# Token sums moved to VectorE, score blocks of 512 and 256 columns, and new numbers in a scheduling table, in a fused attention and two-layer feed-forward kernel

## The chip, the cores and the metric

The kernel runs on 1 core of one Trainium2 chip. The metric is the device time of one execution in microseconds (us). The time before is 764.21 us, the median of 3 runs (762.48 to 764.49). The profiler shows one execution on that core, engine by engine: TensorE (PE, and PEld for its weight loads), VectorE (DVE), ScalarE (ACT), GpSimd (POOL) and SyncE (SP, whose queue issues nearly all DMAs).

## The reference

Attention over 2 x 8 heads, 768 tokens, head size 64, where a query sees only keys of its own hash bucket (6 sign bits of a projection). Its output is 1536 tokens of 512 values, which pass through two feed-forward layers, each 512 to 2048 to 512. All in float32.

```python
mask = q_bucket[:, :, :, None] == k_bucket[:, :, None, :]
scores = np.where(mask, scale * q @ k.T, -1e9)
attn = np.exp(scores - max) / (sum + 1e-9)
x = (attn @ v)                       # as (1536, 512)
h = x @ w_in1;  x = (h * np.tanh(softplus(h))) @ w_out1
h = x @ w_in2;  out = (h - np.tanh(h)) @ w_out2
```

The weights w_in and w_out arrive as float64 (512 KB for each 128 x 512 tile) and are turned into float32 in the kernel.

## The kernel before

**Numbers in two parts.** A matrix product keeps float32 accuracy by splitting each operand into a rounded part and a remainder (names ending in h and l) and adding three products (L969 to L971, L1033, L1034, L1046), or two where one operand is exact.

**Attention.** Eight pairs of heads, one after the other. A pair's q, k and v are loaded, split (L404 to L424), and stacked by SP DMAs into operands a, b, c, d, in which the bucket's bits ride along. For each of 96 blocks of 128 queries TensorE makes 768 scores in four matmuls (L551, L552) into a PSUM tile `s` of two banks, with 384 columns in each bank. There is one such tile (`ps_s`, one buffer); three early blocks use two ordinary banks in its place (`SPLIT_S`). VectorE clamps the scores and takes their minimum (L555), ScalarE takes the exponential and the row sums (L577), TensorE transposes (L612), ScalarE rounds the result to `ph` (L628), VectorE makes the remainder `pl` (L631), and TensorE multiplies both with v (L590, L591). For some chunks GpSimd makes `ph` and `pl` (L355, L624). At the end of a half, 1/sum goes to DRAM and comes back spread over partitions (`inv`, `r`, L670, L674), and the result is scaled and split into `xh`, `xl` (L688 to L695).

**Feed-forward layers.** Each layer works on two halves of 768 tokens (one per batch entry), each in 8 units of 256 hidden columns. A unit's first product runs in seven block products in the manner of Strassen, from sums of weight blocks (`f`, L769) and sums of token blocks (t2, t3, t4, from the `tokens` function). In the first half of layer 1 it runs in eight plain products. The sums of tokens are 16 instructions per half (`whole` and `diff`, L855 and L858 in the source, recorded under the helper's line L769 as `t<-xh,xl` and `t<-t`), for three halves, all on GpSimd. Rounding a result is ACT work, its remainder (`gl`, `a`, `o`) VectorE work. The second product (L1033, L1034 in layer 1, L1046 in layer 2) sums over all units into six PSUM banks; its first two tiles are the two halves of the tile `s`. At the end `keep` writes xh and xl of layer 1, and `leave` copies each output tile out of PSUM (L1082) and sends it off.

**Weights.** `to_float` loads a float64 tile into a `raw` buffer (4 of them) and converts it: L792, L800 and L812 on VectorE, L808 on ScalarE. For the first two units of layer 1 the last step (L812) is GpSimd's; these eight tiles are converted during attention, one each 14 ticks of 1.13 us from tick 60 on (`CONV_A`, `CONV_S`). From the third unit on, the times follow the unit's own (`CONV1`), and all is VectorE's.

**What sets the order.** Every step is an `op` with an engine, a cost, a key (its due time) and a latency. `Plan.order` is a list scheduler: it plays the engines forward by these numbers, takes at each moment the op that can start first (lowest key among equals), and the instructions are then issued to each engine in that order. On the chip each engine runs its own list in order and waits at an instruction until its inputs and buffers are there. So a cost or latency in the table changes only the order. A DMA is an op of an engine "DMA" with cost max(0.55, bytes / 180e3 per us) and a latency of 2.1 us; on the chip that is the SP queue, which issues in order.

Of the kernel before, what the change touches and what calls it, by code (L numbers as in the profile page):

```python
# [30 lines left out]
U32 = mybir.dt.uint32  # L31
# [17 lines left out]
T_BUFS, P_BUFS, U_BUFS = 4, 6, 3  # L49
RAW_BUFS = 4  # L50

# [6 lines left out]
LATE = 0.22  # L58
# [20 lines left out]
RAW = 12.0  # L79
# [12 lines left out]
CONV2 = 6.0  # L92
N_PRE = 2
PLAIN = 8
TOK_A = 0.0
TOK_L = 75.0
TOK_S = 1.3
TOK_T = 3.0
CONV_A = 60
CONV_S = 14  # L100
CONV_R = 15.0
# [28 lines left out]
class Plan:  # L130


    LAT = {"PE": 0.2, "DMA": 2.1, "-": 0.0}

# [7 lines left out]
    def buf(self, pool, tag, shape, dtype=F32):  # L142
        return Buf(self, pool, tag, shape, dtype)

    def op(self, eng, cost, key, fn, reads=(), writes=(), after=(), release=0.0, lat=None):
        o = Op()
        o.lat = self.LAT.get(eng, LATE) if lat is None else lat
# [113 lines left out]
def tile_lsh_attention_moe(  # L261
# [96 lines left out]

    def dma(nbytes, key, out, in_, reads=(), writes=(), release=0.0, rate=180e3):

        op("DMA", max(0.55, nbytes / rate), key, lambda: nc.sync.dma_start(out=out(), in_=in_()), reads, writes, release=release)

# [173 lines left out]
    def scores(g, h, half, t, key):  # L536
# [4 lines left out]
        used = slice(0, NR + D) if g or h else slice(0, P)  # L541
        p, mn = buf("p", "p", [P, 2, HB]), buf("small", "mn", [P, 1])
        sm = sums[g, half]
        rows = (False, True) if g or h else (False, True, "bits")
        reads = [(x, y, half) for x in (a, c_) for y in rows]
        reads += [(x, y, i) for x in (b_, d_) for y in rows for i in range(2)]

        def products(outs):
            for kk, o in outs:
                kc = slice(kk * HB, (kk + 1) * HB)  # L550
                nc.tensor.matmul(o, a()[:, tok], b_()[:, kc], start=True, stop=False)  # L551
                nc.tensor.matmul(o, c_()[used, tok], d_()[used, kc], start=False, stop=True)  # L552
# [6 lines left out]
        if n in SPLIT_S:  # L559

            lows = []
            for kk in range(2):
                sc, low = buf("ps_t", "pt", [P, 512]), buf("small", "mn2", [P, 1])
                op("PE", 0.35, key, lambda sc=sc, kk=kk: products([(kk, sc()[:, :HB])]), reads, [sc])
                op("DVE", 0.47, key + 0.1, lambda sc=sc, kk=kk, low=low: clamp(p()[:, kk], sc()[:, :HB], low()), [sc], [(p, kk), low])
                lows.append(low)
            op(
                "DVE", 0.07, key + 0.15,
                lambda: nc.vector.tensor_tensor(out=mn(), in0=lows[0](), in1=lows[1](), op=ALU.min), lows, [mn],
            )  # L570
        else:
            sc = buf("ps_s", "s", [P, 2, 512])
            op("PE", 0.7, key, lambda: products([(kk, sc()[:, kk, 0:HB]) for kk in range(2)]), reads, [sc])
            op("DVE", 0.87, key + 0.1, lambda: clamp(p(), sc()[:, :, 0:HB], mn()), [sc], [(p, 0), (p, 1), mn])
        op(
# [23 lines left out]
    def chunk(g, h, half, c, ps, o, key, done):  # L599
# [9 lines left out]
        def transpose(ts):  # L609
            for t in ts:  # L610
                pc = ps[t]().rearrange("p a b -> p (a b)")
                nc.tensor.transpose(pt()[:, t * P:(t + 1) * P], pc[:, c * P:(c + 1) * P], ident)  # L612

        op("PE", 0.33, key, lambda: transpose(range(TB)), ps, [(pt, 0), (pt, 1)])
        if len(queue) >= PV_LAG:
# [34 lines left out]
    def inverse(g, half, key):  # L650
# [24 lines left out]

        op("DMA", 0.3, key + 0.3, store, [rt], [("inv", g, half)])
        op("DMA", 0.6, key + 0.4, spread, [("inv", g, half)], [r])

# [103 lines left out]
    def to_float(w, m, key, t, tok, lead=0.0, pooled=False):  # L782
# [3 lines left out]
        def word(i):  # L786
            return raw().bitcast(U32).rearrange("p (n t) -> p n t", t=2)[:, :, i]

        dma(P * DM * 8, key - RAW, raw, lambda: w[m], [], [raw], release=key - RAW - 4.0 - lead, rate=FAST)
        op(  # L790
            "DVE", 0.4, key,
            lambda: nc.vector.tensor_scalar(  # L792
# [41 lines left out]
    def tokens(layer, sb, keys, slack):  # L834
# [5 lines left out]
        for name in ("t2", "t3", "t4"):  # L840
            hl = [buf(f"t{sb + 1}", f"{name}{x}", [P, 2, HB], F32R) for x in "hl"]
            ops[name] = (lambda n, k, hl=hl: hl[n]()[:, k]), [(b, k) for b in hl for k in range(2)]
            more.append(hl)
        gate = [] if sb == 0 else ["wd"]
        for k in range(2):
            x = [buf("t", "t", [P, XB], F32) for i in range(4)]
# [6 lines left out]
            def whole(name, i, key, k=k, x=x, tmp=tmp):  # L853
                at_ = ops[name][0]
                op("POOL", 1.0, key, lambda: add(nc.gpsimd, tmp(i), at_(0, k), at_(1, k)), [*x_of(name), *gate], [x[i]], release=key - slack)  # L855

            def diff(i, a, b, key, x=x, tmp=tmp):
                op("POOL", 1.0, key, lambda: add(nc.gpsimd, tmp(i), tmp(a), tmp(b), True), [x[a], x[b]], [x[i]])  # L858

# [30 lines left out]
    def unit_weights(layer, sb, u, plain):  # L890
# [5 lines left out]
        for part in range(2):  # L896
# [3 lines left out]
            if (layer, sb) == (1, 0):  # L900
                for side in range(2):
# [3 lines left out]
                        weights[1][part], 2 * u + side, when,  # L905
                        lambda part=part, side=side: w32[part]()[:, side].bitcast(U32), (w32[part], side), lead=CONV_R if n < N_PRE else 0.0, pooled=n < N_PRE,
                    )
# [45 lines left out]
    def unit(layer, sb, u, ops):  # L953
# [7 lines left out]
        def product(a, b, bank, start, k):  # L961
# [10 lines left out]

            op("PE", 1.06, k, emit, [(tl, 0), (tl, 1), *toks], [bank])

# [3 lines left out]
        def act(src, m, i, k):  # L978
# [44 lines left out]
    def outer1(m, g, w, acc, key, d):  # L1023
# [26 lines left out]
    def keep(sb, acc, key):  # L1050

        for d in range(KD):
            for (a, n), cols, t0, nt in (
# [17 lines left out]
    def leave(sb, acc, key):  # L1071
        for t, (a, n_) in enumerate(acc):
# [120 lines left out]
```

## Time and profile before

| | before |
|---|---|
| median of 3 runs | 764.21 us |
| the profiled execution, its time | 763.45 us |
| its span, first to last instruction | 761.7 us |
| granted TensorE clock, mean | 0.997 |
| busy: PE, DVE, ACT, POOL | 743.0, 616.6, 513.9, 240.0 us |
| DMA moved | 111.09 MB |

The profiled execution took 763.45 us, 1.75 us more than its span; these lie around the first and last instruction. It is 0.76 us under the median of the three runs. Attention fills the span up to about 250 us (its last products stand beside the first unit of layer 1), layer 1 reaches to about 510 us and layer 2 to the end. A busy time is an average: where an engine is waited for is read from the idle time that stands in brackets behind a row of the timeline, and from the table of waits.

### The profile page before, as it was taken

The numbers are of one execution on the slowest core, as the hardware profiler recorded it, in microseconds if no ns is written. First come the engines' busy times: TensorE is split into PE (matmuls) and PEld (weight loads), VectorE is DVE, ScalarE is ACT, GpSimd is POOL, SyncE is SP. The second block draws the span as 40 slices with busy tenths as digits, with TensorE's granted clock in tenths as the row PEclk, the third lists the DMA queues.
The fourth block names the chain that finished last, engine by engine and source line by source line (L and its number), as shares of the span: only waits on it lengthen the run. The fifth ranks groups of instructions, "written<-read, shape, count | busy, mean of one in ns | idle before, by whom it ended". The sixth has DMA issues, their size and how long they took to land.

```text
span 761.7 us, 12370 instructions
## 1 busy us (share of the span) xinstructions
PE 743.0 (98%) x4189; PEld 678.2 (89%) x4189; DVE 616.6 (81%) x1220; ACT 513.9 (67%) x1076; POOL 240.0 (32%) x258
## 2 busy tenths in 40 slices
PE   7999999999997999999999999999999999999997
PEld 5898989999986999999999999998998898888986
DVE  6899999999999787877699999889987567665542
ACT  6999899999986765455575766666656455554541
POOL 5687697887745003700002231002530000000000
PEclk9999999999999999999999999999999999999999
DMA  6586686785452377525646555664312114120002
GB/s 175 146 209 173 160 207 195 199 203 152 108 168 95 115 252 231 190 107 191 217 162 210 190 191 211 223 205 138 111 56 83 56 56 167 64 75 28 28 0 83
DMA packets 40172, 111.09 MB, mean 146 GB/s; under 512 B 6310, under 2 KB 9254, under 8 KB 40108
## 3 DMA queue, kind: packets, MB, share of 16 engines
q1 hardware_dynamic: 39532, 109.67, 47.8%
q8 instruction: 33, 0.54, 0.3%
q10 hardware_dynamic: 576, 0.62, 0.2%
q14 instruction: 31, 0.25, 0.1%
HBM read 71.40 MB, written 19.97 MB: 120 GB/s over the span
## 4 chain that ended last, share of the span: by engine, by line
PE 85%; DVE 7%; DMA 3%; ACT 2%; issue 2%; POOL 0%; SPq 0%; ACTq 0%; POOLq 0%; DVEq 0%
PE pt L1046 11%; PE pt L969 10%; PE pt L971 10%; PE pt L970 10%; PE pt L612 7%; PE pt L1034 6%; PE s L1033 6%; PE pt L1033 5%; PE s L1046 5%; PE s L551 4%; PE s L552 3%; PE pt L590 3%; PE pt L591 3%; DVE p L555 2%; DVE pl L631 1%
## 5 line engine op out<-in xcount | busy, mean ns | idle before, releaser
L769 POOL TENSOR_TENSOR t<-xh,xl 128x384 f32<-128x384 f32 x24 | 42.5, 1774 | 254.0 <-DVE o L769 77.3
L969 PE MATMUL pt<-xh,a 128*128 128x384 f32 x320 | 108.2, 338 | 1.1 <-ACT pl L983 0.5
L971 PE MATMUL pt<-xh,a 128*128 128x384 f32 x320 | 107.9, 337 | 0.0
L970 PE MATMUL pt<-xl,a 128*128 128x384 f32 x320 | 107.8, 337 | 0.0
L577 ACT ACTIVATE p<-p,mn 128x768 f32<-128x768 f32 x96 | 90.5, 943 | 5.7 <-DVE p L555 3.9
L555 DVE TENSOR_SCALAR_CACHE_REDUCE p<-s 128x768 f32<-128x768 f32 x93 | 88.2, 949 | 7.0 <-PE s L552 6.1
L612 PE MATMUL pt<-cst,p 128*128 128x128 f32 x576 | 88.5, 273 | 3.4 <-ACT p L577 1.9
L612 PEld LDWEIGHTS pt<-cst,p 128*128 128x128 f32 x576 | 71.5, 140 | 11.7 <-ACT p L577 3.8
L631 DVE TENSOR_TENSOR pl<-pt,ph 128x384 fp32r<-128x384 f32 x148 | 78.0, 545 | 4.6 <-ACT ph L628 3.4
L769 DVE TENSOR_TENSOR gl<-pl,gh 128x384 fp32r<-128x384 f32 x128 | 73.5, 580 | 9.6 <-ACT gh L988 9.2
L1046 PE MATMUL pt<-o,gh 128*128 128x512 f32 x256 | 79.6, 392 | 0.0
L628 ACT CAST ph<-pt 128x384 fp32r<-128x384 f32 x148 | 67.8, 480 | 14.8 <-PE pt L612 6.9
L590 PE MATMUL pt<-ph,vt 128*128 128x384 f32 x192 | 72.0, 375 | 1.6 <-DVE pl L631 1.4
L551 PE MATMUL s<-b,a 128*128 128x384 f32 x186 | 68.7, 369 | 3.2 <-DVE p L555 3.0
L1034 PE MATMUL pt<-gh,o 128*128 128x256 f32 x256 | 71.7, 280 | 0.0
L988 ACT CAST gh<-pl 128x384 fp32r<-128x384 f32 x128 | 64.8, 512 | 7.4 <-DVE pl L769 6.7
L591 PE MATMUL pt<-pl,vt 128*128 128x384 f32 x192 | 65.3, 340 | 2.2 <-DVE pl L631 2.1
L969 PEld LDWEIGHTS pt<-xh,a 128*128 128x128 f32 x320 | 60.3, 189 | 6.6 <-DVE pl L769 0.9
L552 PE MATMUL s<-d,c 77*128 77x384 f32 (+1 forms) x186 | 63.2, 340 | 0.0
L970 PEld LDWEIGHTS pt<-xl,a 128*128 128x128 f32 x320 | 60.5, 189 | 1.8
L971 PEld LDWEIGHTS pt<-xh,a 128*128 128x128 f32 x320 | 60.5, 189 | 0.0
L769 DVE TENSOR_TENSOR pl<-pt,f 128x384 f32<-128x384 f32 x32 | 17.8, 556 | 46.8 <-ACT f L986 46.7
(154 smaller groups left out, 1960.4 us busy)
## 6 DMA issues: line engine op xcount, KB each, us to landing
w<-w SPq DMA_DIRECT2D x64, 512.0 KB
raw<-in_moe_w_in_dram SPq DMA_DIRECT2D x32, 512.0 KB
raw<-in_moe_w_out_dram SPq DMA_DIRECT2D x32, 512.0 KB
w<-t SPq DMA_DIRECT2D x32, 256.0 KB
b<-kh SPq DMA_DIRECT2D x30, 192.0 KB
v<-in_v_dram SPq DMA_DIRECT2D x8, 384.0 KB
r<-inv SPq DMA_DIRECT2D x32, 96.0 KB
a<-qh SPq DMA_DIRECT2D x15, 192.0 KB
```

Source lines behind the costliest of these rows:

```text
L551: nc.tensor.matmul(o, a()[:, tok], b_()[:, kc], start=True, stop=False)
L555: nc.vector.tensor_scalar(out=out, in0=in_, scalar1=MASKED, scalar2=None, op0=ALU.min, op1=ALU.min, accum_out=low)
L577: lambda: nc.scalar.activation(out=p(), in_=p(), func=AF.Exp, bias=mn(), scale=-1.0, accum_out=sm()[:, h, t:t + 1],),
L590: nc.tensor.matmul(o()[:, :HB], vt()[:, c, :], ph()[:, :HB], start=(c == 0), stop=False)
L591: nc.tensor.matmul(o()[:, :HB], vt()[:, c, :], pl()[:, :HB], start=False, stop=(c == NT - 1))
L612: nc.tensor.transpose(pt()[:, t * P:(t + 1) * P], pc[:, c * P:(c + 1) * P], ident)
L769: eng.tensor_tensor(out=out, in0=in0, in1=in1, op=ALU.subtract if sub else ALU.add)
L969: nc.tensor.matmul(o, tl()[:, 0, c], at_(0, kk), start=start and kk == 0, stop=False, skip_group_check=not start)
L970: nc.tensor.matmul(o, tl()[:, 0, c], at_(1, kk), start=False, stop=False, skip_group_check=not start)
L971: nc.tensor.matmul(o, tl()[:, 1, c], at_(0, kk), start=False, stop=kk == 1, skip_group_check=not start)
L1034: nc.tensor.matmul(r()[:, 0, rest], w()[:, y, c], flat[x][:, SEG:], start=st and d % 2 == 0, stop=sp, skip_group_check=True)
L1046: nc.tensor.matmul(o, x()[:, i, c], w()[:, y], start=m == 0 and k == 0, stop=m == KF - 1 and k == 2)
```

## The change

All sums of tokens are made on VectorE. A block's 768 scores are made as 512 and 256 columns, so that they lie without a gap in the two banks; the three early blocks that use ordinary banks are divided in the same way. In the last unit of a half the accumulators are finished in the order 0, 2, 1, 3, 4, 5, and copied out in that order. There are 5 `raw` buffers. The eight tiles converted during attention are due from tick 10 on, one each 22 ticks. In the table, DMA latency is 3.0 (a raw load's 4.0), the rate 250e3 bytes per us, and the four stores and two loads of `inv` count 1.3 and 1.2 for 0.3 and 0.6; a few costs of other ops change by some hundredths (such hunks are left out below).

```diff
-RAW_BUFS = 4
+RAW_BUFS = 5
+RAW_LAT = 4.0
+RATE, ISSUE = 250e3, 0.55
+C_STORE, C_SPREAD = 1.3, 1.2
+LAT_DMA = 3.0
+TOKS = ("DVE", 0.47)
...
-CONV_A = 60
-CONV_S = 14
+CONV_A = 10
+CONV_S = 22
...
+        parts = (slice(0, XB), slice(XB, S))
+
         def products(outs):
-            for kk, o in outs:
-                kc = slice(kk * HB, (kk + 1) * HB)
+            for kc, o in outs:
                 nc.tensor.matmul(o, a()[:, tok], b_()[:, kc], start=True, stop=False)
                 nc.tensor.matmul(o, c_()[used, tok], d_()[used, kc], start=False, stop=True)
...
-            op("PE", 0.7, key, lambda: products([(kk, sc()[:, kk, 0:HB]) for kk in range(2)]), reads, [sc])
-            op("DVE", 0.87, key + 0.1, lambda: clamp(p(), sc()[:, :, 0:HB], mn()), [sc], [(p, 0), (p, 1), mn])
+            flat = lambda: sc().rearrange("p a b -> p (a b)")
+            op("PE", 0.69, key, lambda: products([(kc, flat()[:, kc]) for kc in parts]), reads, [sc])
+            op("DVE", 0.87, key + 0.1, lambda: clamp(p(), flat()[:, :S], mn()), [sc], [(p, 0), (p, 1), mn])
...
-        op("DMA", 0.3, key + 0.3, store, [rt], [("inv", g, half)])
-        op("DMA", 0.6, key + 0.4, spread, [("inv", g, half)], [r])
+        op("DMA", C_STORE, key + 0.3, store, [rt], [("inv", g, half)])
+        op("DMA", C_SPREAD, key + 0.4, spread, [("inv", g, half)], [r])
...
+    LAST = (0, 2, 1, 3, 4, 5)
...
+        et = nc.vector if TOKS[0] == "DVE" else nc.gpsimd
...
-                op("POOL", 1.0, key, lambda: add(nc.gpsimd, tmp(i), at_(0, k), at_(1, k)), [*x_of(name), *gate], [x[i]], release=key - slack)
+                op(*TOKS, key, lambda: add(et, tmp(i), at_(0, k), at_(1, k)), [*x_of(name), *gate], [x[i]], release=key - slack)
...
-                op("POOL", 1.0, key, lambda: add(nc.gpsimd, tmp(i), tmp(a), tmp(b), True), [x[a], x[b]], [x[i]])
+                op(*TOKS, key, lambda: add(et, tmp(i), tmp(a), tmp(b), True), [x[a], x[b]], [x[i]])
...
-            k = key + 1.38 * t
+            k = key + 1.38 * LAST[t]
...
-                    k = key + dt * (n_out * i + t if u < NU - 1 else 2 * t + i)
+                    k = key + dt * (n_out * i + t if u < NU - 1 else 2 * LAST[t] + i)
```

The order that comes out differs in many places. Three of them follow, each before and after.

GpSimd before, from its last work of attention on: `ph` and `pl` are the last chunk's, and behind them stand the first sums of tokens, with nothing in between.

```order
L355 TENSOR_SCALAR ph<-f 128x384
L624 TENSOR_TENSOR pl<-f,ph 128x384
L769 TENSOR_TENSOR t<-xh_131,xl_135 128x384 x2
L769 TENSOR_TENSOR t<-t 128x384
L769 TENSOR_TENSOR t<-xh_133,xl_137 128x384
L769 TENSOR_TENSOR t<-t 128x384 x2
```

VectorE after, in layer 1: a piece of its list with two of these sums (`t<-xh,xl` and `t<-t`), among conversions of weights (L800, L808, L820) and remainders (`gl`, `o`).

```order
L777 TENSOR_TENSOR gl<-pl,gh 128x384
L800 TENSOR_SCALAR w_4824<-raw 128x512
L777 TENSOR_TENSOR o_4820<-w_4509,o_4820 128x512
L808 SCALAR_TENSOR_TENSOR w_4824<-raw,w_4824 128x512
L800 TENSOR_SCALAR w_4843<-raw 128x512
L777 TENSOR_TENSOR t<-xh_133,xl_137 128x384
L808 SCALAR_TENSOR_TENSOR w_4843<-raw,w_4843 128x512
L777 TENSOR_TENSOR t<-t 128x384
L777 TENSOR_TENSOR gl<-pl,gh 128x384
```

The sums have left GpSimd's list, which now ends with the last chunk's `pl`; on VectorE they stand in layer 1, behind the end of attention.

SyncE's queue from its first DMA on, before: the first pair's k and v, the stacking of `b`, and the second pair's k.

```order
L361 DMA k<-in_k_dram 128x384 x2
L361 DMA v<-in_v_dram 128x768
L361 DMA b<-kh 64x768 x2
L361 DMA k<-in_k_dram 128x768
L361 DMA a<-qh 64x768
L361 DMA q<-in_q_dram 128x768
```

The same place after:

```order
L367 DMA k<-in_k_dram 128x384 x2
L367 DMA v<-in_v_dram 128x768
L367 DMA raw<-in_moe_w_in_dram 128x512
L367 DMA b<-kh 64x768 x2
L367 DMA k<-in_k_dram 128x768
L367 DMA a<-qh 64x768
```

A raw load of 512 KB now stands ahead of the first stack and of the second pair's k.

TensorE's last unit, before: its first accumulators, of which the first two are halves of the tile `s` (o_9190 and o_9235 are the two weight tiles of the unit).

```order
L1046 MATMUL s<-o_9235,gh 128x512 x2
L1046 MATMUL s<-o_9235,gl 128x512
L1046 MATMUL s<-o_9190,gh 128x512 x2
L1046 MATMUL s<-o_9190,gl 128x512
L1046 MATMUL s<-o_9235,gh 128x512 x2
L1046 MATMUL s<-o_9235,gl 128x512
L1046 MATMUL pt<-o_9190,gh 128x512 x2
L1046 MATMUL pt<-o_9190,gl 128x512
```

And after:

```order
L1055 MATMUL s<-o_9235,gh 128x512 x2
L1055 MATMUL s<-o_9235,gl 128x512
L1055 MATMUL pt<-o_9190,gh 128x512 x2
L1055 MATMUL pt<-o_9190,gl 128x512
L1055 MATMUL pt<-o_9235,gh 128x512 x2
L1055 MATMUL pt<-o_9235,gl 128x512
L1055 MATMUL s<-o_9190,gh 128x512 x2
L1055 MATMUL s<-o_9190,gl 128x512
```

Between the first half of `s` and its second half now stand the six matmuls of an accumulator in another bank.

## Rows read from the trace of the kernel before

**Rows 1.** The page, part 1: busy us (share of the span) x instructions.

```profile
PE 743.0 (98%) x4189; PEld 678.2 (89%) x4189; DVE 616.6 (81%) x1220; ACT 513.9 (67%) x1076; POOL 240.0 (32%) x258
```

**Rows 2.** Windows: stretch, its length, busy us (instructions) by engine; PEclk; DMA.

```profile
core 0: us, PE busy (x) PEld busy (x) DVE busy (x) ACT busy (x) POOL busy (x), PEclk, DMA share, GB/s
0.00:16.00 16.00, 11.91 (x48) 8.29 (x49) 10.42 (x26) 9.73 (x18) 7.33 (x17) 1.00 0.71 197
16.00:236.00 220.00, 215.61 (x1386) 198.37 (x1384) 206.77 (x458) 202.33 (x443) 160.58 (x193) 1.00 0.65 167
236.00:247.00 11.00, 6.88 (x43) 5.74 (x41) 10.82 (x17) 5.34 (x13) 10.60 (x10) 1.00 0.45 142
247.00:262.00 15.00, 13.90 (x69) 13.58 (x70) 11.16 (x21) 10.00 (x20) 0.78 (x1) 0.89 0.39 133
400.00:460.00 60.00, 60.00 (x348) 56.30 (x347) 56.93 (x94) 39.42 (x83) 19.17 (x16) 1.00 0.61 200
520.00:560.00 40.00, 39.54 (x196) 35.02 (x195) 39.29 (x67) 23.82 (x50) 18.33 (x14) 1.00 0.36 119
```

**Rows 3.** Waits of PE from 236 to 258: total us, times, longest.

```profile
PE pt L591 <- DVE pl L631: 2.1, 1, 2.1
PE pt L590 <- DVE pl L631: 1.4, 1, 1.4
PE pt L612 <- DVE pl L631: 1.3, 1, 1.3
```

**Rows 4.** Timeline of DVE, 238 to 247: start us, us, instruction.

```profile
238.27 1.38 DVE L800 SCALAR_TENSOR_TENSOR w<-raw,w 128x512 uint32<-128x512 uint32 x1
...
239.70 1.10 DVE L792 TENSOR_SCALAR w<-raw 128x512 uint32<-128x512 uint32 x1
...
241.66 1.51 DVE L812 CUSTOM_DVE_ANT_0 w<-raw,w 128x1024 uint16<-128x1024 uint16 x1
...
244.25 1.40 DVE L800 SCALAR_TENSOR_TENSOR w<-raw,w 128x512 uint32<-128x512 uint32 x1
245.57 1.34 DVE L688 TENSOR_TENSOR u<-u,r 128x384 f32<-128x384 f32 x1
```

**Rows 5.** Timeline of POOL, first and last token sums of that stretch.

```profile
237.83 2.68 POOL L769 TENSOR_TENSOR t<-xh,xl 128x384 f32<-128x384 f32 x2
...
246.58 1.20 POOL L769 TENSOR_TENSOR t<-t 128x384 f32<-128x384 f32 x1
```

**Rows 6.** Timeline of DVE, the same instructions at other moments.

```profile
229.86 0.42 DVE L792 TENSOR_SCALAR w<-raw 128x512 uint32<-128x512 uint32 x1
...
231.30 0.69 DVE L800 SCALAR_TENSOR_TENSOR w<-raw,w 128x512 uint32<-128x512 uint32 x1
...
235.72 0.68 DVE L812 CUSTOM_DVE_ANT_0 w<-raw,w 128x1024 uint16<-128x1024 uint16 x1
...
254.62 0.55 DVE L688 TENSOR_TENSOR u<-u,r 128x384 f32<-128x384 f32 x1
```

**Rows 7.** Groups by form: count | busy us, mean ns | idle before.

```profile
L1034 PE MATMUL pt<-gh,o 128*128 128x256 f32 x256 | 71.7, 280 | 0.0
...
L970 PE MATMUL pt<-xl,a 128*128 128x384 f32 x320 | 107.8, 337 | 0.0
...
L1033 PE MATMUL pt<-gh,o 128*128 128x512 f32 x128 | 47.2, 391 | 0.0
...
L769 POOL TENSOR_TENSOR t<-xh,xl 128x384 f32<-128x384 f32 x24 | 42.5, 1774 | 254.0 <-DVE o L769 77.3 <-DVE f L769 68.1 <-DVE xl L769 54.8
...
L769 POOL TENSOR_TENSOR t<-t 128x384 f32<-128x384 f32 x24 | 28.0, 1166 | 1.9
...
L769 DVE TENSOR_TENSOR pl<-ph,f 128x384 f32<-128x384 f32 x32 | 18.5, 578 | 3.1 <-ACT f L986 3.1
```

**Rows 8.** The chain that ended last, early and at 236: start us, us, what.

```profile
8.58 4.75 DMA k<-in_k_dram
...
236.46 3.26 DMA raw<-in_moe_w_in_dram
```

**Rows 9.** Timeline of PE, last unit: a row with the idle time before it.

```profile
751.73 0.73 PE L1046 MATMUL s<-o,gh 128*128 128x512 f32 x2 [0.68 <-ACT t L1082]
```

More of the change, by code (lines that the diff above doesn't have):

```diff
@@ L93 @@
 N_PRE = 2
+POOLED = True
 PLAIN = 8
@@ L130 @@
 class Plan:
-    LAT = {"PE": 0.2, "DMA": 2.1, "-": 0.0}
+    LAT = {"PE": 0.2, "-": 0.0}
     def __init__(self):
@@ L146, in op @@
         o = Op()
-        o.lat = self.LAT.get(eng, LATE) if lat is None else lat
+        o.lat = (LAT_DMA if eng == "DMA" else self.LAT.get(eng, LATE)) if lat is None else lat
         o.n, o.eng, o.cost, o.key, o.fn = len(self.ops), eng, cost, key, fn
@@ L357, in pool_copy, with dma @@
         )
-    def dma(nbytes, key, out, in_, reads=(), writes=(), release=0.0, rate=180e3):
-        op("DMA", max(0.55, nbytes / rate), key, lambda: nc.sync.dma_start(out=out(), in_=in_()), reads, writes, release=release)
+    def dma(nbytes, key, out, in_, reads=(), writes=(), release=0.0, rate=None, lat=None):
+        op("DMA", max(ISSUE, nbytes / (rate or RATE)), key, lambda: nc.sync.dma_start(out=out(), in_=in_()), reads, writes, release=release, lat=lat)
     pairs = [(b, hp) for b in range(B) for hp in range(NP)]
@@ L541, in scores @@
         used = slice(0, NR + D) if g or h else slice(0, P)
-        p, mn = buf("p", "p", [P, 2, HB]), buf("small", "mn", [P, 1])
+        p, mn = buf("p", "p", [P, S]), buf("small", "mn", [P, 1])
         sm = sums[g, half]
@@ L561, in scores @@
             lows = []
[L562 to L565, printed above, removed]
+            for kk, kc in enumerate(parts):
+                sc, low, w = buf("ps_t", "pt", [P, 512]), buf("small", "mn2", [P, 1]), kc.stop - kc.start
+                op("PE", 0.46 * w / XB, key, lambda sc=sc, kc=kc, w=w: products([(kc, sc()[:, :w])]), reads, [sc])
+                op("DVE", 0.08 + w * 0.00103, key + 0.1, lambda sc=sc, kc=kc, w=w, low=low: clamp(p()[:, kc], sc()[:, :w], low()), [sc], [(p, kk), low])
                 lows.append(low)
@@ L610, in transpose @@
             for t in ts:
-                pc = ps[t]().rearrange("p a b -> p (a b)")
-                nc.tensor.transpose(pt()[:, t * P:(t + 1) * P], pc[:, c * P:(c + 1) * P], ident)
-        op("PE", 0.33, key, lambda: transpose(range(TB)), ps, [(pt, 0), (pt, 1)])
+                nc.tensor.transpose(pt()[:, t * P:(t + 1) * P], ps[t]()[:, c * P:(c + 1) * P], ident)
+        op("PE", 0.327, key, lambda: transpose(range(TB)), ps, [(pt, 0), (pt, 1)])
         if len(queue) >= PV_LAG:
@@ L787, in word @@
             return raw().bitcast(U32).rearrange("p (n t) -> p n t", t=2)[:, :, i]
-        dma(P * DM * 8, key - RAW, raw, lambda: w[m], [], [raw], release=key - RAW - 4.0 - lead, rate=FAST)
+        dma(P * DM * 8, key - RAW, raw, lambda: w[m], [], [raw], release=key - RAW - 4.0 - lead, rate=FAST, lat=RAW_LAT)
         op(
-            "DVE", 0.4, key,
+            "DVE", 0.34, key,
             lambda: nc.vector.tensor_scalar(
@@ L905, in unit_weights @@
                         weights[1][part], 2 * u + side, when,
-                        lambda part=part, side=side: w32[part]()[:, side].bitcast(U32), (w32[part], side), lead=CONV_R if n < N_PRE else 0.0, pooled=n < N_PRE,
+                        lambda part=part, side=side: w32[part]()[:, side].bitcast(U32), (w32[part], side), lead=CONV_R if n < N_PRE else 0.0, pooled=POOLED and n < N_PRE,
                     )
@@ L971, in emit @@
                     nc.tensor.matmul(o, tl()[:, 1, c], at_(0, kk), start=False, stop=kk == 1, skip_group_check=not start)
-            op("PE", 1.06, k, emit, [(tl, 0), (tl, 1), *toks], [bank])
+            op("PE", 1.045, k, emit, [(tl, 0), (tl, 1), *toks], [bank])
         def plus(out, bank, x, k):
@@ L982, in act @@
             if layer == 1:
-                op("ACT", 0.45, k - URG, lambda: nc.scalar.activation(out=y()[:, W], in_=src()[:, W], func=AF.Mish), [src, "wd"], [y])
+                op("ACT", 0.39, k - URG, lambda: nc.scalar.activation(out=y()[:, W], in_=src()[:, W], func=AF.Mish), [src, "wd"], [y])
             else:
@@ L1034, in emit @@
                 nc.tensor.matmul(r()[:, 0, rest], w()[:, y, c], flat[x][:, SEG:], start=st and d % 2 == 0, stop=sp, skip_group_check=True)
-        op("PE", 1.05, key, emit, [(gh, 0), (gh, 1), (gl, 0), (gl, 1), (w, 0), (w, 1)], [(a, n), (r, 0)])
+        op("PE", 1.04, key, emit, [(gh, 0), (gh, 1), (gl, 0), (gl, 1), (w, 0), (w, 1)], [(a, n), (r, 0)])
     def outer2(m, g, w, acc, key, t):
@@ L1059, in keep @@
                 to = slice(x0 * P, (x0 + nt) * P)
-                k = key + 2.1 * d
+                k = key + 2.1 * LAST[d]
                 op(
```

## The prediction

> **What bounds the kernel now.** I read the busy shares first, then the same by stretch, then the waits and the timeline of the one stretch in which TensorE idles most, and the rows around it. TensorE is busy for 743.0 of 761.7 us [rows 1], so nothing can be won beyond its 18.7 us of idle time and whatever it runs at the lower clock. By stretch [rows 2] this time lies in four places: the first 16 us (4.09 us idle), attention from 16 to 236 (4.39 us in 220), the passage from attention to layer 1 (4.12 us from 236 to 247, then 1.10 us to 262, at a mean granted clock of 0.89), and the very end. In the layers it is nearly nothing: 0.00 us from 400 to 460 and 0.46 us from 520 to 560.
>
> The passage is the dearest stretch and VectorE bounds it: it is busy for 10.82 of 11 us [rows 2], and the three waits of TensorE there, 2.1, 1.4 and 1.3 us, all end with a `pl` that VectorE makes [rows 3]. The reader is to see in the timeline why: five VectorE instructions take 1.38, 1.10, 1.51, 1.40 and 1.34 us [rows 4], and their like at other moments 0.69, 0.42, 0.68, 0.69 and 0.55 [rows 6]. While they run GpSimd is in its first eight sums of tokens, from 237.83 to 247.78 [rows 5], work for a later half of layer 1 that GpSimd begins because its list holds nothing else.
>
> **The sums of tokens.** With the sums gone from GpSimd the five instructions should take what they take elsewhere: 0.69 + 0.68 + 0.83 + 0.71 + 0.79 = 3.70 us less on the engine that TensorE waits for. The ends: nothing (if something else is late in their place), and 4.8 us of waits [rows 3] with the clock on top. The clock: after TensorE had waited its 2.1 us, the stretch 247 to 262 shows 0.89 as its mean, between full speed (2.4 GHz) and the lower level of 1.2, which is 0.11 x 15 = 1.65 us of full-speed time lost [rows 2]. With shorter waits I count half of it back, 0.8. I take 3.7 + 0.8 = 4.5 us of the possible 6.45. Late next would be the last chunk's `ph` from ScalarE, and the raw load below.
>
> The Trainium skill (SBUF — State Buffer, "Who interferes with whom") says that VectorE and GpSimd share one pair of ports as an exclusive lock: the instruction that comes second is held until the first has ended, and a VectorE instruction with two SBUF inputs is among those that can be held. The trace agrees in kind, with 3.70 us over five instructions. If each were held for a whole sum, an estimate of (247.78 - 237.83) / 8 = 1.24 us, the relief would be 6.2 us, all 4.8 us of waits would go and the sum below would be about 1.1 us lower; the rows show less, and I keep to them.
>
> The 48 sums now cost VectorE time. The nearest row is VectorE's own difference of two such tiles, 578 ns [rows 7], so 48 x 0.578 = 27.7 us in place of 70.5 us of GpSimd (42.5 + 28.0, [rows 7]). Against it stands what they cost VectorE before by stretching others: 3.70 / 8 = 0.46 us a sum, 22 us for all 48. That is even within 6 us over 500 us of layers in which TensorE hardly waits, so I count nothing against it; what it costs without that cover is a rival below. From 520 to 560, where VectorE has 39.29 of 40 us and TensorE 0.46 us of idle time, the fifth raw buffer may bring loads forward: -0.2 us, with -0.46 as its end on that side.
>
> **The start.** A raw load now stands in SP's queue ahead of the stack of `b` and of the second pair's k, and its first conversion, an L792 of 0.42 us [rows 6], stands on VectorE ahead of the first clamp. Queued behind the load are two stacks and that k, for which GpSimd waits; k already takes 4.75 us to land, and a raw load alone takes 3.26 [rows 8]. Queued behind the conversion is everything VectorE does for the first blocks. The ends are 0 (the load lands in time and the 0.42 us fall into a wait of ScalarE) and 3.26 + 0.42 + 0.69 = 4.4 us. VectorE's 0.42 us I count in full, and 0.6 of the load's, because TensorE's idle 4.09 us of these first 16 hides some of it: +1.0 us.
>
> **Attention.** The new latencies and due times reorder it everywhere, and no row shows the new order's waits. TensorE idles for 4.39 us there [rows 2]; a new order can remove at most that, and I bound a loss by the same number. Eight conversions are spread from the start on, where before they sat in the later part; that evens VectorE's load of 206.77 us in 220. I take -0.5 us.
>
> **Scores of 512 and 256 columns.** The columns are the same 768, twice. A 512 and a 256 take 391 + 280 ns, two of 384 take 2 x 337 = 674 [rows 7]; 3 ns by 192 such pairs is 0.6 us either way, and I take 0. VectorE's clamp reads the same 768 columns.
>
> **The last tiles.** TensorE waits 0.68 us for a copy of the first half of `s` before it may write the second [rows 9]. Now six matmuls of another bank stand between, and two alone show 0.73 us [rows 9], more than that wait. Nothing else is late before the last tile: -0.7 us, at worst 0.
>
> **The sum.** -4.5 + 1.0 - 0.5 - 0.2 + 0 - 0.7 = -4.9 us. The profiled execution took 763.45 us, so 758.55. It lies 0.76 us under the median of its three runs; the median after may stand to this sum likewise or not, so I add half, 0.35, and say 758.9.
>
> **The rivals.**
>
> *The passage stays as it is.* Then another wait stands where the slow VectorE instructions stood. The chain speaks for it: it puts 3.26 us from 236.46 on a raw load [rows 8], not on VectorE. Against it: that load lands at 239.72, and the instruction which the chain hands it to had begun at 239.70 [rows 4], straight after one that ended at 238.27 + 1.38 = 239.65; it did not wait. If it holds nevertheless, only the end is won and the start cancels it or not: 763.45 - 0.7 + 0.35 = 763.1.
>
> *More falls than I count.* All 4.8 us of waits and the 1.65 us of clock, attention's 4.39, 0.46 and 0.68 go, and the start costs 0.42: -11.6, so 752.2 with the same 0.35. For it speaks that VectorE is nearly as full in attention (206.77 of 220 us, [rows 2]) as in the passage, so that what relieves or evens it there may count too; against it, that no order removes all idle time.
>
> *VectorE overflows in the layers (slower).* Its place is layer 1's second half and the first of layer 2. From 400 to 460 VectorE has 3.07 us free, from 520 to 560 0.71 us [rows 2]. The 16 sums of the one and the 14 of the other (all GpSimd instructions there) cost 9.25 and 8.1 us. If nothing of the stretched time comes back, 6.2 and 7.4 us do not fit, 13.6 in all. If half comes back, 6.8 us reach TensorE through `gl` and the weight tiles: 758.9 + 6.8 = 765.7, and in full 772.5. It decides from 4.9 us on. Against it stands the 0.46 us per sum from [rows 4, 5], by which 7.4 and 6.4 us come back and only about 1 us does not fit.
>
> The Trainium skill (Perfetto Trace Analysis, "Optimizing Scalar/DVE Operations") speaks for this rival: where VectorE is saturated, work may better go to other engines, even to GpSimd, though it adds that the two share a port and the move might not help. Here VectorE is saturated; which half of that sentence holds is what the layers will show.
>
> **How the numbers follow.** The forecast has a chance of 0.55, with a range of its own of 756.3 to 761.6. The larger gain has 0.17, the unchanged passage 0.15, the overflow 0.13. What can be told from no change is about 0.3%, 2.3 us: faster means under 761.9, slower over 766.5. Faster: the forecast nearly whole (0.53) and the larger gain, 0.70. Within: the unchanged passage and the rest of the forecast, and the milder part of the overflow, 0.20. Slower: the rest of the overflow, and a start that costs its 4.4 us with a worse order of attention, 0.10. The range of 754.0 to 765.5 leaves out the lower part of the larger gain and most of the overflow.
>
> **What would show it.** In the changed kernel's profile GpSimd should have no instruction after its last `pl`; the L800, L808, L820 and L695 of VectorE near the end of attention should take about 0.42, 0.69, 0.68 and 0.55 us; the waits of TensorE for `pl` in the passage should add up to 1 to 1.5 us in place of 4.8, and the clock there be near 1.00. The sums on VectorE should take about 0.58 us each, with TensorE at 0 to 0.5 us of idle time in the layers. TensorE should start the second half of `s` in the last unit without idle time. The second pair's k should land later than 13.3 us. The forecast is wrong if the passage keeps waits of 3 us or more, if the layers show TensorE idle for more than 2 us, or if attention's idle time moves by more than 2.

## The result and the profile after

The changed kernel takes 756.4 us (median of 4 runs, 756.1 to 757.5), the kernel before 763.9 beside it: a ratio of 0.991, with an interval of 0.989 to 0.9925. The profiled execution took 756.07 us with a span of 754.3. 758.9 was predicted, inside a range of 754.0 to 765.5.

The busy shares and the windows of the changed kernel, in the columns of [rows 1, 2]:

```profile
PE 738.6 (98%) x4189; PEld 669.9 (89%) x4189; DVE 611.7 (81%) x1268; ACT 514.2 (68%) x1076; POOL 170.1 (23%) x210
...
0.00:16.00 16.00, 11.45 (x44) 7.49 (x45) 11.14 (x28) 9.47 (x18) 7.05 (x15) 1.00 0.81 223
16.00:236.00 220.00, 215.12 (x1393) 193.08 (x1392) 206.37 (x457) 202.25 (x441) 161.54 (x194) 1.00 0.65 166
236.00:247.00 11.00, 9.41 (x57) 8.15 (x56) 10.91 (x24) 7.58 (x16) 1.54 (x2) 1.00 0.60 204
247.00:262.00 15.00, 14.49 (x83) 13.84 (x83) 11.87 (x24) 13.19 (x27) 0.00 (x0) 1.00 0.46 149
...
520.00:560.00 40.00, 40.00 (x202) 36.11 (x201) 35.33 (x73) 23.94 (x50) 0.00 (x0) 1.00 0.34 111
```

From 236 to 262 us TensorE idles for (11 - 9.41) + (15 - 14.49) = 2.10 us, where before it was 4.12 + 1.10 = 5.22 [rows 2], and the clock is at 1.00 throughout: 3.1 us of idle time are back, and by the estimate of the prediction (0.11 x 15) 1.65 us of clock. VectorE is as full as before in the first stretch (10.91 of 11 us), but it does 24 instructions there in place of 17. The rows of its timeline that answer to [rows 4], and TensorE's waits that answer to [rows 3]:

```profile
237.18 1.03 DVE L820 CUSTOM_DVE_ANT_0 w<-raw,w 128x1024 uint16<-128x1024 uint16 x1
...
238.67 0.42 DVE L800 TENSOR_SCALAR w<-raw 128x512 uint32<-128x512 uint32 x1
...
239.12 0.69 DVE L808 SCALAR_TENSOR_TENSOR w<-raw,w 128x512 uint32<-128x512 uint32 x1
...
243.00 0.55 DVE L695 TENSOR_TENSOR u<-u,r 128x384 f32<-128x384 f32 x1
```

```profile
PE pt L619 <- DVE pl L638: 0.8, 1, 0.8
PE pt L598 <- DVE pl L638: 0.8, 1, 0.8
PE pt L978 <- ACT pl L992: 0.5, 1, 0.5
```

The one instruction still long (1.03) runs beside GpSimd's last `ph` and `pl`, at 236.04 to 237.66. On VectorE the sums cost what an undisturbed difference costs, 0.55 us each:

```profile
L777 DVE TENSOR_TENSOR t<-t 128x384 f32<-128x384 f32 x24 | 13.2, 551 | 0.1
L777 DVE TENSOR_TENSOR t<-xh,xl 128x384 f32<-128x384 f32 x24 | 13.2, 550 | 0.0
```

To see where the time went I compare when TensorE begins the same instruction in both traces. Layer 1's first product (ahead of it stand the same matmuls in both) begins 0.7 us earlier, the first outer product of layer 1 then 5.4 earlier (before, then after):

```profile
221.14 0.33 PE L969 MATMUL pt<-xh,a 128*128 128x384 f32 x1
...
263.43 0.39 PE L1033 MATMUL s<-gh,o 128*128 128x512 f32 x1
```

```profile
220.46 0.33 PE L978 MATMUL pt<-xh,a 128*128 128x384 f32 x1
...
258.03 0.39 PE L1042 MATMUL s<-gh,o 128*128 128x512 f32 x1
```

So the passage brings 5.4 - 0.7 = 4.7 us. The lead stays at 5.4 to 5.5 through layer 1, grows to 7.0 from 474 to 560 us (the turn from layer 1 to layer 2), stays there, and is 7.4 at the end. Ahead of layer 1 it changes sign: the first pair's last transposes begin 2.2 us later (before, then after).

```profile
41.36 0.49 PE L612 MATMUL pt<-cst,p 128*128 128x128 f32 x3
```

```profile
43.55 0.49 PE L619 MATMUL pt<-cst,p 128*128 128x128 f32 x3
```

But by then the changed kernel has also done the four matmuls of one more block of scores, which take 0.7 us (36.91 to 37.61 in the trace before). So the start costs 1.5 us, and the rest of attention gives 2.2 back.

### The profile page after: what moved, and what is told of

Its sections match the earlier page's. It is cut to its first block, busy times and chain, and to the rows that moved or that the text cites. A ratio compares the mean times of both kernels' runs of the same rounds, so it can differ in the third digit from the quotient of the medians.

```text
span 754.3 us, 12351 instructions
## 1 busy us (share of the span) xinstructions
PE 738.6 (98%) x4189; PEld 669.9 (89%) x4189; DVE 611.7 (81%) x1268; ACT 514.2 (68%) x1076; POOL 170.1 (23%) x210
## 4 chain that ended last, share of the span: by engine, by line
PE 89%; DVE 4%; DMA 2%; ACT 2%; issue 1%; POOL 0%; SPq 0%; ACTq 0%; DVEq 0%; POOLq 0%
PE pt L1055 12%; PE pt L980 10%; PE pt L979 10%; PE pt L978 10%; PE pt L619 7%; PE pt L1043 6%; PE s L1055 6%; PE s L1042 6%; PE pt L1042 6%; PE s L558 4%; PE s L559 4%; PE pt L598 3%; PE pt L599 3%; DVE p L562 2%; DMA k<-in_k_dram 1%
## 5 line engine op out<-in xcount | busy, mean ns | idle before, releaser
L619 PE MATMUL pt<-cst,p 128*128 128x128 f32 x576 | 86.6, 273 | 2.6 <-ACT p L585 1.6
L777 DVE TENSOR_TENSOR gl<-pl,gh 128x384 fp32r<-128x384 f32 x128 | 69.9, 552 | 14.7 <-ACT gh L997 14.1
L619 PEld LDWEIGHTS pt<-cst,p 128*128 128x128 f32 x576 | 69.9, 140 | 9.2 <-ACT p L585 2.5
L558 PE MATMUL s<-b,a 128*128 128x512 f32 (+1 forms) x186 | 68.0, 366 | 3.6 <-DVE p L562 3.3
L559 PE MATMUL s<-d,c 77*128 77x512 f32 (+3 forms) x186 | 59.3, 340 | 0.4 <-DVE d L439 0.4
L992 ACT ACTIVATE pl<-pt 128x384 f32<-128x384 f32 x48 | 23.5, 493 | 48.6 <-PE pt L980 48.3
```

What stands on the lines that cost most here:

```text
L619: nc.tensor.transpose(pt()[:, t * P:(t + 1) * P], ps[t]()[:, c * P:(c + 1) * P], ident)
```

## The experiments

Two theories stood against each other. The first: GpSimd's sums stretch VectorE's instructions, and that costs wherever VectorE is the late engine, at the passage and at the turn. The second: the table (raw buffers, delays, earlier conversions) reorders the work, and the engine of the sums does not matter. Ratios are to the kernel before.

**The sums alone, both ways.** `a_pool` is the changed kernel with the sums issued on GpSimd again, `b_toks` the kernel before with the sums on VectorE, planned at 0.47 us.

```diff
 a_pool, from the changed kernel
-        et = nc.vector if TOKS[0] == "DVE" else nc.gpsimd
+        et = nc.gpsimd
 b_toks, from the kernel before (the same in diff())
-                op("POOL", 1.0, key, lambda: add(nc.gpsimd, tmp(i), ...
+                op("DVE", 0.47, key, lambda: add(nc.vector, tmp(i), ...
```

> The changed kernel with its token sums issued on GpSimd again, every other instruction and its order as in the changed kernel. Theory 1 (GpSimd's sums stretch VectorE's conversions, and these hold TensorE at the passage from attention to layer 1 and at the turn from layer 1 to 2): the sums run at about 237 to 248 us again, VectorE's instructions of that stretch take 1.0 to 1.5 us in place of 0.4 to 0.7, the first outer product of layer 1 comes 3 to 4.5 us later than in the changed kernel (261 to 262.5 us in place of 258.0), the turn gives back 0.5 to 1.5 us, and the time is 760 to 762.5 us. Theory 2 (the new table, its raw buffers, delays and earlier conversions, brought the gain, and the sums' engine does not matter): within 1 us of 756.4.

> The kernel before with the one edit that VectorE makes the token sums (at 0.47 us each in the order's plan); table, score blocks and last tiles as before. Theory 1: passage 4 to 5 us shorter, turn 0.5 to 1.5 us shorter, the time 757.5 to 759.5, so that this edit alone holds three quarters of the gain or more. Theory 2: 762 to 764.5, the gain needs the table.

`a_pool` took 764.4 us, ratio 1.0009 (0.9999 to 1.0019): the whole gain is gone, somewhat more than expected. `b_toks` took 757.8, ratio 0.9925 (0.9908 to 0.9941): 6 of the 7.4 us, as expected. In `a_pool` the conversions and a weight tile of VectorE are long again, beside sums of GpSimd that run from 237.64 to 247.92; its timeline (DVE, then the first outer product):

```profile
239.48 1.39 DVE L808 SCALAR_TENSOR_TENSOR w<-raw,w 128x512 uint32<-128x512 uint32 x1
...
240.92 0.97 DVE L638 TENSOR_TENSOR pl<-pt,ph 128x384 fp32r<-128x384 f32 x2
241.82 1.16 DVE L800 TENSOR_SCALAR w<-raw 128x512 uint32<-128x512 uint32 x1
...
245.57 1.49 DVE L808 SCALAR_TENSOR_TENSOR w<-raw,w 128x512 uint32<-128x512 uint32 x1
246.98 1.49 DVE L777 TENSOR_TENSOR a<-w,a 128x512 fp32r<-128x512 f32 x1
```

```profile
263.96 0.39 PE L1042 MATMUL s<-gh,o 128*128 128x512 f32 x1
```

TensorE's program and every other engine's order are those of the changed kernel, nothing but GpSimd reads these sums before 294 us, and still TensorE comes 5.9 us later. The second theory falls. The 5.9 us are not all waiting: in the columns of [rows 2],

```profile
236.00:247.00 11.00, 8.81 (x47) 7.33 (x45) 10.90 (x19) 6.61 (x15) 10.54 (x10) 0.88 0.57 201
247.00:262.00 15.00, 12.99 (x59) 12.36 (x59) 9.78 (x18) 8.28 (x18) 0.92 (x1) 0.75 0.34 113
```

TensorE's idle time is 2.19 + 2.01 = 4.20 us, 2.1 more than in the changed kernel and less than the 5.22 before. The other 3.8 us come with the clock, whose mean as a share of full speed (2.4 GHz, the lower level is 1.2) is 0.88 and 0.75 here: at most 0.12 x 11 + 0.25 x 15 = 5.1 us of full-speed time, some of it idle anyway. So what the waits cost depends on how long TensorE then runs at the lower level, and the clock can be the larger part. In the layers the loss is in one place, the turn, where TensorE is busy for 37.92 of the 40 us from 520 to 560 and falls back by 2.7 us against the changed kernel.

**The same sums, later.** `b_hold` leaves them on GpSimd but lets them begin only after attention's last tile.

```diff
+    if (layer, sb, name, k) == (1, 1, "b12", 0):
+        nc.gpsimd.tensor_copy(mark[:, 0:1], xl[KD - 1][:, B * S - 1:B * S])
     add(nc.gpsimd, tmp(i), at_(0, k), at_(1, k))
```

> The kernel before with one more GpSimd instruction, a copy of one column out of the last tile that attention writes, ahead of GpSimd's first token sum: the sums are the same but cannot begin before attention has ended (about 250 us). Order otherwise unchanged. Theory 1: VectorE's five instructions of 237 to 247 us fall to 0.4 to 0.7 us each, TensorE's three waits there (4.8 us together) fall to 1 to 2, and the first outer product comes 3 to 4.5 us earlier than in the kernel before (259 to 260.5 us in place of 263.4); the sums stretch VectorE's instructions after 250 us instead, where TensorE has work queued, which may return up to 1 us; the time is 759 to 761. Theory 2: the passage keeps its waits and the time stays within 0.7 us of 763.9.

The passage did as the first theory says, and the total did not: 764.6 us, ratio 1.0008 (0.9996 to 1.0019). The first outer product comes at 257.73, 5.7 us earlier than before. Then the sums run from 251.29 on, VectorE's `gl` and `o` take twice their time, and TensorE waits for them (PE, DVE):

```profile
257.73 0.39 PE L1038 MATMUL s<-gh,o 128*128 128x512 f32 x1
...
262.31 0.79 PE L1038 MATMUL s<-gl,o 128*128 128x512 f32 x1 [3.72 <-DVE gl L769]
```

```profile
256.19 1.50 DVE L769 TENSOR_TENSOR o<-w,o 128x512 fp32r<-128x512 f32 x1
257.61 1.37 DVE L769 TENSOR_TENSOR gl<-pl,gh 128x384 fp32r<-128x384 f32 x1
258.90 1.48 DVE L769 TENSOR_TENSOR o<-w,o 128x512 fp32r<-128x512 f32 x1
...
261.70 0.55 DVE L769 TENSOR_TENSOR gl<-pl,gh 128x384 fp32r<-128x384 f32 x1
```

The `gl` of 0.55 us begins after the last sum has ended at 261.23. I had expected TensorE to have work queued there; it had not. With this wait the clock falls as well, to a mean of 0.96 from 247 to 262 us and 0.93 from there to 300, and by 281 us TensorE is 0.8 us behind the kernel before:

```profile
262.00:300.00 38.00, 37.70 (x203) 35.11 (x204) 32.23 (x60) 22.18 (x43) 2.81 (x1) 0.93 0.70 230
```

The wait was moved by 20 us, not removed, which speaks for the stretching once more, and against moving the sums to this later place.

**The last tiles.** `b_last` is the kernel before with the order 0, 2, 1 alone, `a_nolast` the changed kernel without it, `c_two` the kernel before with this order and the sums on VectorE.

```diff
+    LAST = (0, 2, 1, 3, 4, 5)
-    k = key + 2.1 * d  ...  k = key + 1.38 * t  ...  else 2 * t + i)
+    k = key + 2.1 * LAST[d]  ...  k = key + 1.38 * LAST[t]  ...  else 2 * LAST[t] + i)
```

> The kernel before with the order 0, 2, 1 of the last tiles alone. If the tail and the turns gain by it as I worked out (TensorE no longer waits at the wide score bank's two halves at a turn), the time falls by 0.4 to 1.0 us, and none of the difference lies ahead of 360 us. Rival: the turn's gain of 1.5 us between layers 1 and 2 comes from this edit and not from the sums; then the time falls by 1.8 to 2.5 us.

> The changed kernel with the last tiles in order 0, 1, 2, 3, 4, 5 again. Theory 1: TensorE waits again between the two halves of the wide score bank at the end, 0.7 to 1.0 us, nothing at the turn; 757.1 to 757.5 us. Rival: the order 0, 2, 1 costs at the turn what it brings at the end; within 0.3 us of 756.4.

> The kernel before with two edits, the token sums on VectorE and the order 0, 2, 1 of the last tiles; table and score blocks as before. The sums alone gave 757.8 us, the last tiles alone moved nothing in the total: their gain of 1.0 us at the end was lost at the turn from layer 1 to 2, where TensorE waited 2.0 us while GpSimd's sums ran. Theory 1 (a sum on GpSimd costs wherever VectorE is the late one; with the sums gone the turn is quiet in any order): the end's 1.0 us adds to the sums', 756.5 to 757.0, so that the table and the score blocks are worth 0 to 0.5 us. Theory 2 (the table earns its share in attention): 757.5 to 758, and the changed kernel's 756.4 needs the table.

`b_last` 763.7 us, ratio 1.0001 (0.9987 to 1.0015): nothing. `a_nolast` 758.0, ratio 0.993 (0.9918 to 0.9943), 1.5 us over the changed kernel where 0.7 to 1.0 were expected. `c_two` 757.5, ratio 0.9922 (0.991 to 0.9934), half a us above what I had expected. From the start of the last `pt<-xh,a` matmul of layer 2 (743.20 before, 736.18 after) to TensorE's end (758.15, 750.16) the traces are alike to 0.01 us: 13.98 us in every kernel with the new order, 14.95 in every one without, so the order is worth 0.97 us on TensorE. `a_nolast` shows the wait of [rows 9] again:

```profile
746.14 0.73 PE L1055 MATMUL s<-o,gh 128*128 128x512 f32 x2 [0.68 <-ACT t L1091]
```

`b_last` loses 1.2 us at the turn, behind VectorE stretched by GpSimd's sums (PE, DVE, POOL):

```profile
533.64 0.45 PE L970 MATMUL pt<-xh,a 128*128 128x384 f32 x1 [1.79 <-DVE pl L770]
```

```profile
530.47 1.24 DVE L793 TENSOR_SCALAR t<-raw 128x512 uint32<-128x512 uint32 x1
531.75 1.36 DVE L801 SCALAR_TENSOR_TENSOR t<-raw,t 128x512 uint32<-128x512 uint32 x1
533.04 0.55 DVE L770 TENSOR_TENSOR pl<-pt,f 128x384 f32<-128x384 f32 x1
```

```profile
530.31 1.11 POOL L770 TENSOR_TENSOR t<-xh,xl 128x384 f32<-128x384 f32 x1 [0.98 <-DVE t L801]
```

So neither theory of `b_last` was right as written: the tail gains, and the turn takes it back as long as the sums are on GpSimd (in `c_two`, with the sums on VectorE, the turn gains 0.8 us, as in `b_toks`).

**The score blocks.** `a_384` computes the scores in two blocks of 384 columns again; `a_384b` is the same once more, beside `a_again`, the changed kernel unaltered.

```diff
-        parts = (slice(0, XB), slice(XB, S))
+        parts = (slice(0, HB), slice(HB, S))
```

> The changed kernel with scores computed in two blocks of 384 columns again, in two banks, order of the instructions as the plan then gives it. If the blocks are worth nothing in time, as I worked out (the same 768 columns, one matmul more or less of fixed cost either way): within 0.6 us of 756.4. Rival: blocks of 512 and 256 save TensorE time in attention or at the weight loads, then 757.5 or more.

> The changed kernel once more, with nothing altered, beside the next run: the two blocks of 384 columns gave 755.6 us against 756.4 here although TensorE reached each point of the program within 0.2 us of the changed kernel. If the blocks are worth nothing, both land within 0.4 us of each other on one chip; rival: 512 and 256 columns cost 0.5 to 1 us.

> The changed kernel with scores in two blocks of 384 columns, once more. Blocks worth nothing: within 0.4 us of the changed kernel beside it, thus 755.5 to 756.5. Rival: 0.5 to 1 us faster than it.

755.6 us at first, ratio 0.9898 (0.9885 to 0.991), which looked like a gain; then 757.1, ratio 0.9913 (0.9893 to 0.9932), beside 756.8, ratio 0.9911 (0.9893 to 0.993), for the changed kernel. The blocks are worth nothing that can be measured. Two measurements of one and the same kernel lie 1.5 us apart here. Of the 1.3 us between their profiled executions the clock can account for all: from 17 to 21 us its mean is 0.57 in `a_384b` and 1.00 in `a_384` (0.43 x 4 = 1.7 us). TensorE's start times vary by 0.7 us between the two profiles of the changed kernel. Differences of that size, in what follows and in `a_nolast` and `c_two`, rest on the rows, not on the totals.

**The table.** `a_conv` puts the early conversions back to their old times, `a_lat` the delays and rates, `a_late384` tries a time between with blocks of 384.

```diff
 a_conv
-CONV_A = 10, CONV_S = 22
+CONV_A = 60, CONV_S = 14
 a_lat
-RAW_LAT = 4.0; RATE = 250e3; C_STORE, C_SPREAD = 1.3, 1.2; LAT_DMA = 3.0
+RAW_LAT = 2.1; RATE = 180e3; C_STORE, C_SPREAD = 0.3, 0.6; LAT_DMA = 2.1
 a_late384, from a_384
-CONV_A = 10, CONV_S = 22, CONV_R = 15.0
+CONV_A = 24, CONV_S = 20, CONV_R = 2.0
```

> The changed kernel with the first conversions of weights at their old times (the first after 60 ticks, then every 14, in place of 10 and 22). Theory 1 (the early raw load in front of the first stacks costs about 2 us up to the end of the first head pair, and the spread of the conversions gives about as much back later in attention): the first pair ends at 41.4 us in place of 43.8, the last pairs as late or later, and the time is 755.5 to 757.5. Rival (the start's cost is a loss that nothing returns): 754 to 755 us.

> The changed kernel with the plan's old delays and rates of transfers (2.1 us and 180 GB/s for all, 0.3 and 0.6 us for the two small ones), conversions early as in the changed kernel. If the counted delays bring attention's gain (its last transposes of pair 7 at 211.7 us), these come 1 to 2 us later and the time is 757 to 759; rival: the conversions' times alone make it, within 0.6 us of 756.4.

> Blocks of 384 columns, and the early conversions put a little later: the first after 24 ticks, then every 20, released no more than 2 us ahead, so that the first raw load stands behind the first copies of the next stack in SyncE's queue and not before them. If the start's cost comes from that load and from the conversion ahead of VectorE's first score work, the first pair ends about 2 us earlier than in the changed kernel (41.4 to 42 us in place of 43.8) and, if the rest stays, the time is 753.5 to 755. Rival: as with the old times of the conversions, later pairs take it back, 756 to 758.

`a_conv` 757.9 us, ratio 0.9928 (0.9915 to 0.9941); `a_lat` 756.5, ratio 0.991 (0.9891 to 0.993); `a_late384` 759.8, ratio 0.995 (0.9934 to 0.9966). The delays are worth nothing in the total, against my expectation. The early conversions cost at the start and seem to earn as much or more later: in `a_conv` the last transposes of the first pair come at 42.23 in place of 43.55 (1.3 us, where 2.4 were expected), and TensorE's waits from 16 to 58 us fall from 2.1 to 1.1 us (changed kernel, then `a_conv`):

```profile
PE pt L599 <- POOL pl L631: 0.6, 1, 0.6
PE s L558 <- DVE p L562: 0.6, 2, 0.3
PE pt L456 <- POOL kl L430: 0.5, 1, 0.5
PE pt L456 <- DVE ql L420: 0.2, 1, 0.2
PE pt L598 <- DVE p L562: 0.2, 1, 0.2
```

```profile
PE pt L599 <- POOL pl L631: 0.6, 1, 0.6
PE pt L456 <- POOL kl L430: 0.3, 1, 0.3
PE pt L598 <- DVE p L562: 0.2, 1, 0.2
```

yet layer 1's first product comes 1.2 us later than in the changed kernel (0.6 later than in `a_again`). `a_lat` keeps the early conversions, and its transposes come at 42.20 all the same: the start's cost needs the new delays too, and there again layer 1 begins no earlier (220.54, changed kernel 220.46). `a_late384` also saves the start (41.95) and loses it all: its first outer product comes at 260.91, after waits of 2.8 us from 226 to 262 for VectorE, GpSimd and ScalarE in turn, with no long VectorE row among them, and more is lost at the turn. No kernel here is measurably faster than the changed one.

## Why the prediction was right, and where it was not

The 756.4 us lie at the lower edge of the forecast's own range, 756.3 to 761.6. In the profiled execution, as gains and losses of TensorE's start times:

| Step | predicted us | measured us |
|---|---|---|
| passage from attention to layer 1 | -4.5 | -4.7 |
| start | +1.0 | +1.5 at the end of the first pair |
| attention after it | -0.5 | -2.2 |
| score blocks | 0 | 0 |
| layers | -0.2 | -1.6 |
| last tiles | -0.7 | -0.97 on TensorE, -0.4 in the span |
| sum | -4.9 | -7.4 |

- *Passage.* Mechanism and size held; `a_pool` takes it away and `b_toks` gives it (its TensorE is busy for 9.95 + 14.46 us of these 26, against 9.41 + 14.49). The split inside was off: the idle time fell by 3.1 in place of 3.7 us, and the clock came back whole, 1.65 in place of 0.8. That the two errors nearly cancel in the 4.5 is luck. Of the waits for VectorE's `pl` 1.6 us are left where I said 1 to 1.5, and 0.5 for ScalarE's is new. The rule of the Trainium skill (SBUF — State Buffer, "Who interferes with whom"), by which a blocked instruction is held for the other's whole run, would have given all 4.8 us of waits; the trace agrees in kind, since VectorE's long instructions are gone with the sums, and shows 3.2 us of those 4.8 gone.
- *Start and attention.* The start's cost was mis-sized, 1.5 for 1.0. The conversion's 0.42 us held: the first clamp begins at 10.86 us in place of 10.49. The load's path did not: the queue reaches the stack of `b` at 7.20 us (7.21 before) and k at 8.50 (8.58), so the load in front held up neither. Nor does the cost fall where I had looked for it: TensorE's idle time in the first 16 us grows by only 0.46 us (4.55, before 4.09). k takes 5.29 us to land in place of 4.75, as far as I had said, but the waits that `a_conv` removes are for VectorE's `p` and `ql` behind the early conversion more than for the load. Attention gives back more than I counted: `a_conv`, which is 1.3 us ahead at the first pair and 1.2 behind at layer 1, points to the spread of the conversions, which I had valued at 0.5 us. Together they moved by -0.7 us in this trace and by -0.03 in `a_again`, where I had said +0.5; that the two misses cancel is luck. The five traces whose attention has the old order on every engine (the kernel before, `b_toks`, `b_hold`, `b_last`, `c_two`) begin layer 1 anywhere from 220.72 to 222.65 us, so scatter is larger than the effect, and the separate sizes are no better known than that. The mark that I had set for a wrong forecast here, 2 us of attention's idle time, was not reached: from 16 to 236 us it is 4.88 us, before 4.39.
- *Layers.* The step that failed most clearly: I priced the turn by its 0.46 us of idle time from 520 to 560, as the most that it could give, and it gave 1.6 us (1.5 in `a_again`). Idle time alone is too small a price, as the row behind this list shows. `b_toks` has 0.8 of the gain, so half comes with the sums. The other half is whole in `a_lat` with the old delays, and smaller with the old order of the last tiles (`a_nolast`, 1.1 in all) or the old times of the conversions (`a_conv`, 1.2 in all); the fifth raw buffer was not tried alone, so its parts stay open.
- *VectorE's load.* I called it even: 27.7 us of sums against 22 of stretching. The sums cost 26.4 us (13.2 + 13.2), and VectorE's busy time fell from 616.6 to 611.7, so 31 us of stretching went, 0.65 us a sum in place of 0.46 (28 us from the kernel before to `b_toks`, 36 from `a_pool` to the changed kernel). The rival of an overflow in the layers, for which the Trainium skill spoke (Perfetto Trace Analysis, "Optimizing Scalar/DVE Operations"), fell: from 520 to 560 VectorE is 4 us emptier than before. The other half of that sentence held, that such a move might not help: GpSimd's share was no relief to VectorE. Its reason, the shared port, no run here shows by itself; the runs show only that the two engines' instructions lengthen each other.
- *Last tiles.* Right on TensorE. The span shows less because the last output landed 2.85 us after it was issued, before 2.24 (span's end less the end of the issue, at 751.44 and 759.43). With the new order it took 2.8 us in `a_again` and `c_two` and 2.2 to 2.3 in the seven others (`b_last` and `a_pool` among them), so the order does not decide it.

`c_two`, which has the two edits that count, and the changed kernel differ by 1 us with overlapping intervals. What the table is worth beyond them is not known better than between 0 and some 1.5 us, and stays open.

The row of the turn in the kernel before whose idle time I had taken for the price:

```profile
533.07 0.45 PE L969 MATMUL pt<-xh,a 128*128 128x384 f32 x1 [0.46 <-DVE pl L769]
```

It begins 0.86 us after the matmul ahead of it (532.21), where two like these otherwise lie 0.23 to 0.24 us apart, so the wait cost 0.6 us and not 0.46. From 474 to 560 us the rows show 0.74 us of idle time before and none after, for a gain of 1.6. The last tiles are alike: 0.68 us of idle time, 0.97 gained.

## What to carry to other kernels

Work that is cheap because its engine is idle can be paid for by another engine: before moving work between GpSimd and VectorE, compare the durations of VectorE's same instructions with and without GpSimd beside them, and add up the difference. Where the late engine changes from stretch to stretch, moving the disturbing work in time only moves the wait. And an edit that shows nothing alone (the last tiles, on the kernel before) can gain once another wait is gone: the rows of `c_two` have its 0.97 us, though the total shows only 0.3 (757.8 to 757.5) and `a_nolast` 1.5. Last, a wait of TensorE is priced too low by its idle time alone: the clock behind it, and the gap to the matmul ahead, belong to it.

## What the runs showed of the hardware

Not every VectorE instruction is stretched. By the groups over the whole run, those that read a PSUM tile keep their mean when GpSimd's sums go, those with SBUF inputs alone get shorter (before, then after; count | busy us, mean ns | idle):

```profile
L769 DVE TENSOR_TENSOR o<-w,o 128x512 fp32r<-128x512 f32 x64 | 46.3, 724 | 7.6 <-ACT o L943 7.4
...
L769 DVE TENSOR_TENSOR ph<-pt,ph 128x384 f32<-128x384 f32 x48 | 26.6, 554 | 7.0 <-ACT ph L1002 6.3 <-PE pt L971 0.5
...
L769 DVE TENSOR_TENSOR f<-w 128x256 f32<-128x256 f32 x48 | 22.4, 466 | 0.8 <-DMA w<-w 0.7
```

```profile
L777 DVE TENSOR_TENSOR o<-w,o 128x512 fp32r<-128x512 f32 x64 | 43.9, 685 | 5.0 <-ACT o L952 4.8
L777 DVE TENSOR_TENSOR ph<-pt,ph 128x384 f32<-128x384 f32 x48 | 26.6, 555 | 7.6 <-ACT ph L1011 5.5 <-PE pt L980 1.7
...
L777 DVE TENSOR_TENSOR f<-w 128x256 f32<-128x256 f32 x48 | 20.0, 417 | 0.0
```

`pl<-pt,ph` in `a_pool` shows the same in the small: 0.97 us for two at 240.92, in the midst of the sums, while its neighbours take twice their time. In the trace before, 13 instructions of the three forms with a PSUM input (`pl<-pt,ph`, `pl<-pt,f`, `ph<-pt,ph`) overlap a sum by more than 0.3 us, and none takes more than 0.56 us; of five such `o<-w,o` the longest takes 1.51.

It also goes the other way. In the kernel before, one sum of GpSimd took 7.82 us (the longest of its group: shortest, median and longest in ns) while VectorE ran back to back at ordinary lengths; it ended only in VectorE's first pause:

```profile
L769 POOL TENSOR_TENSOR t<-xh,xl x5: 992/1439/7820, 237.8 to 298.6; 128x384 f32<-128x384 f32 x5
```

```profile
304.91 0.69 DVE L812 CUSTOM_DVE_ANT_0 w<-raw,w 128x1024 uint16<-128x1024 uint16 x1
306.79 0.94 DVE L792 TENSOR_SCALAR w<-raw 128x512 uint32<-128x512 uint32 x1 [1.20 <-issue]
```

That sum began at 298.65 and so ended at 306.47. TensorE lost nothing there: it was busy for all of the 100 us from 300 to 400.
